# Sharing the softmax exponentials between ScalarE and VectorE, and folding the spectral half along both axes

## The chip, the cores and the metric

The kernel runs on one core of a Trainium2 chip. The metric is device time of one execution in microseconds; the median of the runs counts.

## What is computed

Two independent halves are concatenated along the last axis (S = 2048 rows, D = 448 columns each, bf16):

```python
# half A: attention, 16 heads of 28
qkv = x @ wqkv;  q, k, v = split into 16 heads
p = softmax(q k^T * 28**-0.5);  o = p v;  a = o @ wo
# half B: a filter in the frequency domain
X = rfft2(x) ; X = X * (w_r + 1j*w_i) ; b = irfft2(X)      # X is (2048, 225)
out = concatenate([a, b], axis=-1)                          # (2048, 896)
```

In the attention half 16 heads x 2048 x 2048 exponentials are needed, 67 million. That is 1024 *units* of one head, 128 keys and 512 queries (128 partitions x 512 elements).

## The kernel before

**Attention.** Four groups `g` of four heads, four blocks `qc` of 512 queries, sixteen blocks `kc` of 128 keys. `emit_st` (L639) multiplies keys by queries for three units at once: three matmuls with 28 rows each, at row tiles 0, 32, 64 or 96 of the array, each into a PSUM bank of its own out of six; two triples are in flight. `emit_act` (L655) makes one ScalarE exponential over the three banks (128x1536) and writes bf16 to `ET`, a ring of five. `emit_pv` (L662) multiplies the exponentials of four heads by the values: four matmuls with 32 output columns each, at column tiles 0, 32, 64 and 96, accumulated over the 16 key blocks in the bank `ACC`. A column of ones in the values gives the softmax sums; `finish` (L680) copies `ACC` out on VectorE, gathers the sums on TensorE (L702), takes reciprocals (L689), spreads them (L691, L694) and normalises (L698). The output projection is `o_job` (L708, matmuls L711).

**Projections.** Queries and keys (L393) and values (L408) contract over D = 448 as 128 + 128 + 128 + 64 rows, so one matmul in four uses 64 rows. They need x transposed. The first 512 rows are transposed on TensorE (L299), the other 1536 by transposing DMAs (L269).

**Spectral half.** All transforms are matmuls with constant cosine and sine tables. Rows s and s+1024 are added and subtracted on GpSimd first (L358, L361), so even and odd frequencies have half-length sums. `s_job` (L464) transforms along s, `x_job` (L487) along d, `zmul` (L518 to L524, GpSimd) multiplies by W, `y_job` (L554) transforms back along d, `z_job` (L586) back along s. Each of the four takes 128 matmuls. `w_job` (L534) transposes W on TensorE in 64 matmuls, after strided loads into `Wst` (L333 to L347).

**Order of the work.** [...] A planner in the builder (the loop from L809) keeps a clock per engine, with a cost per instruction, and emits TensorE's instructions in one fixed order: a triple of units if its banks are free, a value group if its exponentials are ready, otherwise one step of the job (projection, spectral step or output step) with the smallest due time. Jobs use bank 7 alone until the exponentials are done. The engines then run these fixed orders in sequence and wait on semaphores. If the key or query projection that a triple needs is not done, `force_until` runs it whole, ahead of everything.

The softmax here doesn't subtract the row's maximum and nothing guards it: scores larger than these inputs give would overflow.

## Time and profile before

Median of three runs: 563.34 us (560.5 to 572.84). The profiled execution took 570.4 us.

| engine | busy us | share of the span | instructions |
|---|---|---|---|
| TensorE (PE) | 500.1 | 88% | 3276 matmuls |
| ScalarE (ACT) | 473.6 | 83% | 352 |
| VectorE (DVE) | 132.4 | 23% | 218 |
| GpSimd (POOL) | 87.1 | 15% | 87 |

"Busy" is time in which the engine has an instruction in execution. A busy TensorE is not one at full speed: its clock is granted by a throttle, and the mean grant over this span was 0.844. The chain of work that ended last runs for 44% of the span on TensorE, 28% on ScalarE and 13% on DMA.

### The profile page before, as it was taken

What the parts mean: (1) busy time and instruction counts of PE and PEld (TensorE: products, weight loads), DVE (VectorE), ACT (ScalarE), POOL (GpSimd) and SP (SyncE); (2) the same over time, 40 slices, a digit from 0 to 9 for tenths busy, and PEclk for the clock granted to TensorE, in tenths of its full rate; (3) what the DMA queues carried; (4) which work ended last, traced back from release to release, by engine and by line L of the source; (5) the groups of instructions that cost most, each with busy time, mean ns of one, the idle gap of its engine ahead of it and who ended that gap; (6) DMA issues with size and microseconds to landing.
All of it is one profiled execution on the core that took longest, in us unless ns stands there. A gap on an engine that the chain in (4) does not pass through costs nothing.

```text
span 570.4 us, 7748 instructions
## 1 busy us (share of the span) xinstructions
PE 500.1 (88%) x3276; PEld 164.7 (29%) x3276; DVE 132.4 (23%) x218; ACT 473.6 (83%) x352; POOL 87.1 (15%) x87
## 2 busy tenths in 40 slices
PE   7699795999999999989999899999978888788786
PEld 3222232223333233333333222222222222222222
DVE  2111332212212222122211211213132122222323
ACT  2667895869999999999988579889977559899894
POOL 5038000000000000582505555000000000000000
PEclk9555755659999999999968659789999669999999
DMA  6492130000022022000000000000000011301012
GB/s 167 87 302 81 43 95 16 2 1 0 1 75 75 2 72 75 1 0 2 1 1 0 1 0 1 2 0 1 1 0 1 1 53 55 106 17 41 24 34 80
DMA packets 21394, 21.69 MB, mean 38 GB/s; under 512 B 11792, under 2 KB 19472, under 8 KB 20848
## 3 DMA queue, kind: packets, MB, share of 16 engines
q1 hardware_dynamic: 20208, 19.60, 11.8%
q10 hardware_dynamic: 960, 1.20, 0.7%
q0 software_dynamic: 192, 0.40, 0.3%
q8 instruction: 25, 0.41, 0.3%
q14 instruction: 9, 0.07, 0.1%
HBM read 15.95 MB, written 3.67 MB: 34 GB/s over the span
## 4 chain that ended last, share of the span: by engine, by line
PE 44%; ACT 28%; DMA 13%; issue 6%; DVE 6%; SPq 2%; DVEq 0%; ACTq 0%
ACT ET L659 28%; PE PS L649 11%; PE PS L670 8%; DMA Wst<-in_B_w_r_dram 6%; PE PS L554 5%; PE PS L393 4%; PE PS L487 4%; PE PS L586 3%; PE PS L408 3%; DMA Wst<-in_B_w_i_dram 3%; DMA xAT<-in_A_x_dram 3%; PE PS L464 2%; PE PS L711 1%; DMA R<-in_A_x_dram 1%; DVE R L569 1%
## 5 line engine op out<-in xcount | busy, mean ns | idle before, releaser
L659 ACT ACTIVATE ET<-PS 128x1536 bf16<-128x1536 f32 x342 | 467.3, 1611 | 79.0 <-PE PS L649 78.2
L649 PE MATMUL PS<-qT,kT 28*128 28x512 bf16 x1024 | 149.9, 435 | 26.3 <-ACT ET L659 16.0
L670 PE MATMUL PS<-ET,Vaug 128*32 128x512 bf16 x1024 | 115.4, 444 | 3.7 <-DVE Vaug L255 3.6
L649 PEld LDWEIGHTS PS<-qT,kT 28*128 28x128 bf16 x1024 | 33.6, 92 | 136.1 <-ACT ET L659 98.6
L670 PEld LDWEIGHTS PS<-ET,Vaug 128*32 128x32 bf16 x1024 | 26.5, 95 | 74.2 <-issue 68.4
L487 PE MATMUL PS<-R,T 112*113 112x512 bf16 (+1 forms) x128 | 45.6, 469 | 0.8 <-DVE Vaug L255 0.4
L518 POOL TENSOR_TENSOR ptmp<-R,WT 113x512 f32<-113x512 bf16 (+1 forms) x8 | 9.2, 1153 | 236.4 <-DVE R L500 236.4
L464 PE MATMUL PS<-FR,R 128*112 128x512 bf16 x128 | 39.8, 409 | 1.4 <-DVE R L468 0.5
L554 PE MATMUL PS<-T,R 113*128 113x448 bf16 (+1 forms) x128 | 34.7, 379 | 1.8 <-DVE R L569 0.8
L586 PE MATMUL PS<-R,FR 128*128 128x448 bf16 x128 | 35.1, 391 | 0.9 <-DVE R L569 0.5
L408 PE MATMUL PS<-wst,xAT 128*128 128x112 bf16 (+1 forms) x256 | 33.1, 242 | 2.8 <-DVE astg L598 0.8
L393 PE MATMUL PS<-xAT,wk 128*128 128x512 bf16 x64 | 25.5, 481 | 8.0 <-DMA xAT<-in_A_x_dram 5.6
L393 PE MATMUL PS<-xAT,wq 128*128 128x512 bf16 x64 | 23.3, 451 | 5.1 <-DVE astg L598 1.3
L500 DVE CAST R<-PS 113x512 bf16<-113x512 f32 (+1 forms) x16 | 11.1, 692 | 62.8 <-PE PS L487 33.5
L408 PEld LDWEIGHTS PS<-wst,xAT 128*128 128x128 bf16 (+1 forms) x256 | 18.1, 103 | 23.8 <-issue 8.8
L468 DVE CAST R<-PS 112x512 bf16<-112x512 f32 x16 | 11.1, 692 | 55.7 <-PE PS L464 55.7
L569 DVE CAST R<-PS 128x448 bf16<-128x448 f32 x16 | 10.0, 625 | 52.7 <-PE PS L554 44.1
L487 PEld LDWEIGHTS PS<-R,T 112*113 112x113 bf16 (+1 forms) x128 | 15.4, 151 | 19.5 <-issue 12.5
L255 DVE CAST Vaug<-PS 128x448 bf16<-128x448 f32 x16 | 10.0, 625 | 45.0 <-PE PS L408 45.0
L255 DVE CAST kT<-PS 128x512 bf16<-128x512 f32 x16 | 11.1, 691 | 40.2 <-PE PS L393 40.1
L534 PE MATMUL PS<-cid,Wst 128*113 128x128 bf16 (+1 forms) x64 | 10.8, 307 | 10.5 <-DMA Wst<-in_B_w_i_dram 8.7
L464 PEld LDWEIGHTS PS<-FR,R 128*112 128x112 bf16 x128 | 14.0, 133 | 17.9 <-issue 10.8
(57 smaller groups left out, 263.7 us busy)
## 6 DMA issues: line engine op xcount, KB each, us to landing
FR<-cst_f SPq DMA_DIRECT2D x4, 1024.0 KB, 8.4
FR<-cst_f SPq DMA_DIRECT2D x8, 512.0 KB, 3.6
out_dram<-astg SPq DMA_DIRECT2D x32, 112.0 KB, 1.7
R<-in_B_x_dram SPq DMA_DIRECT2D x2, 896.0 KB, 7.9
T<-cst_t SPq DMA_DIRECT2D x1, 896.0 KB, 4.7
T<-cst_t SPq DMA_DIRECT2D x1, 787.5 KB, 13.6
wst<-in_A_wqkv_dram ACTq DMA_DIRECT2D x1, 672.0 KB, 4.9
Wst<-in_B_w_r_dram SPq DMA_DIRECT2D x2, 225.0 KB, 9.9
```

The costliest lines, as they stand in the source:

```text
L255: P.op(eng, lambda e: e.tensor_copy(dst, src), reads=reads, writes=writes, cost=cost)
L393: mms.append(lambda e, M, c=c, rlo=rlo, rhi=rhi: e.matmul(M, wsb[rlo:rhi, c, g, :], xAT[rlo:rhi, c, 512 * n:512 * (n + 1)], start=(c == 0) ...
L408: mms.append(lambda e, M, c=c, rlo=rlo, rhi=rhi, kq=kq: e.matmul(M[:, 112 * kq:112 * kq + 112], xAT[rlo:rhi, c, 128 * (4 * n + kq):128 * ( ...
L464: mms.append(lambda e, M, c=c: e.matmul(M[0:112, :], src[:, c, 112 * b:112 * b + 112], F1v[:, i, c, :], start=(c == 0), stop=(c == 7)))
L468: P.op("dve", lambda e: e.tensor_copy(Sd[0:112, b, r, 512 * h:512 * h + 512], M[0:112, :]), reads=[mk], writes=[("Sd", h, r, b)], cost=0.68)
L487: mms.append(lambda e, M, ti=ti, part=part, v=v, q=q: e.matmul(M[0:kn, :], T1[0:112, v, q, k0:k0 + kn], Sd[0:112, q, part, 512 * h:512 * h ...
L554: mms.append(lambda e, M, ti=ti, sg=sg, p=p, v=v, b=b, kn=kn: e.matmul(M[:, 0:448], X[0:kn, b, sg, p, ks], T2[0:kn, v, b, :], start=(ti == ...
L569: P.op("dve", lambda e: e.tensor_copy(Y[:, t, r, :], M[:, 0:448]), reads=[mk], writes=[("Y", t, r)], cost=0.6)
L586: mms.append(lambda e, M, r=r, tt=tt, n=n: e.matmul(M[:, 0:448], F2v[:, a % 4, r, tt, :], Y[:, tt, r, :], start=(n == 0), stop=(n == 7)))
L649: ins = e.matmul(bank(u % 6), kT[32 * j:32 * j + DH, g % 2, 128 * kc:128 * (kc + 1)], qT[32 * j:32 * j + DH, g % 2, 512 * qc:512 * (qc + 1 ...
L659: P.op("act", lambda e: e.activation(ET[:, t % NE, 0:n], PS[:, b0:b0 + n], ACT.Exp, scale=scale), reads=[("B", u % 6) for u in us], writes ...
L670: ins = e.matmul(ACC[32 * j:32 * j + 32, :], Vaug[:, g % 2, kc, 32 * j:32 * j + 32], ET[:, t % NE, c0:c0 + 512], start=(kc == 0), stop=(kc ...
```

## The change

The builder is largely rewritten. What it changes on the chip:

1. **Exponentials on VectorE.** Of the 16 key blocks of every query block, blocks 3, 7 and 11 go to VectorE (192 of the 1024 units). The key projection is scaled so that a score arrives as 128 log2(e) times its value. VectorE adds a bias, clamps at zero and writes int16; read as bf16, these bits are a piecewise linear 2^x. Three more copies with 32, 64 and 96 added (shifts by 1/4, 1/2 and 3/4 of an octave) are averaged with it: values scaled by 2^(-c/4) (`Vs`) multiply copy c, so that TensorE sums four value products per such block. ScalarE keeps 13 blocks (832 units), in exponentials of three, two or one bank.
2. **Shared banks and a list scheduler.** All seven banks besides `ACC` serve units of either kind and jobs. VectorE and GpSimd instructions are queued and committed by due time; instructions [...] (`port=True`) are ordered against each other with semaphores.
3. **Column tiles.** Matmuls of jobs are issued as four matmuls of 32 output columns (`cols`), the form that the value products have, rather than one of 128.
4. **Projections** contract over 4 x 112 rows. All of x is loaded in plain layout and transposed on TensorE.
5. **Spectral half folded along both axes.** Rows s, 1024-s, 1024+s, 2048-s and columns d, 448-d are added and subtracted (`fold_chunk`), two chunks on GpSimd, two on VectorE; mirrored rows arrive by indirect DMA (`gather`). Each transform becomes a quarter of its size, with recombination in `zmul` (GpSimd) and `combine` (GpSimd).
6. **W in natural layout**: loaded with frequencies along partitions, the mirrored half with `gather`; no transposes on TensorE.

The aim is to take work from ScalarE and TensorE, at the price of more on VectorE and GpSimd. The core of the diff:

```diff
-        def emit_st(t):
-            us = units(t)
...
+        NB = 4 * NG
+        AQ, DQ = [], []
+        for b in range(NB):
+            for kc in range(16):
+                (DQ if kc in DKS else AQ).append((b, kc))
...
+        def mm(out, lhsT, rhs, start, stop):
+            def full(e):
+                return e.matmul(out, lhsT, rhs, start=start, stop=stop)
+            def cols(e):
+                m = out.shape[0]
+                for c in range(0, m, 32):
+                    c1 = min(c + 32, m)
+                    ins = e.matmul(out[c:c1], lhsT[:, c:c1], rhs, start=start, stop=stop, tile_position=(0, c))
+                return ins
+            return full, cols
...
+        def fill_dve(dsel):
+            for bk, (qi, b, kc, j, slot) in dsel:
+                P.defer("dve", lambda e, bk=bk, slot=slot: e.tensor_scalar(TT[:, 0, slot, :], bank(bk), BIAS, 0.0, ALU.add, ALU.max),
+                        reads=[("B", bk)], writes=[("T", slot)], busy=psum_cost(512), allow=0.8)
+                if slot % 2 == 1:
+                    for c in range(1, NW):
+                        P.defer("dve", lambda e, c=c, slot=slot: e.tensor_scalar(TT[:, c, slot - 1:slot + 1, :], TT[:, 0, slot - 1:slot + 1, :],
+                                                                                 SHF * c, None, ALU.add),
+                                reads=[("T", slot - 1), ("T", slot)], writes=[("T", c, slot // 2)], busy=0.336, allow=3.0, port=True)
...
+            P.op("act", lambda e: e.activation(dst, src, ACT.Exp, scale=ESC), reads=[("B", i) for i in o],
+                 writes=[("E", p + k) for k in range(n)], busy=0.4267 * n + 0.05)
...
+            ncop = 1 if kind == "A" else NW
+            for cc in range(ncop):
...
+                        lh = Vaug[:, g % 2, kc, 32 * j:32 * j + 32] if cc == 0 else Vs[:, g % 2, DKS.index(kc), cc - 1, 32 * j:32 * j + 32]
+                        ins = e.matmul(ACC[32 * j:32 * j + 32, :], lh, rhs, start=first, stop=last, tile_position=(0, 32 * j))
...
-                Wst[:, i, r, :, :], src[h:1024:2, :].rearrange("(t p) k -> p t k", p=128)),
+                P.dma("sp", lambda e, r=r, src=src: e.dma_start(Wn[:, t, 2 * r, :], src[lo:lo + 255:2, :]), "d_wb%d" % t, reads=wdep, writes=[("W", t, r)], kb=56)
+                gather(Wn[:, t, 2 * r + 1, :], src[:, :], 8 + t, "d_wr%d" % t, [("Wr", t, r)], 56, wdep)
...
-        for n, lo, hi in ((1, 512, 1024), (2, 1024, 2048)):
-            for c in range(4):
-                dlo = crow[c][2]
-                P.dma("sp", lambda e, lo=lo, hi=hi, c=c, dlo=dlo: e.dma_start_transpose(xAT[:, c, lo:hi], A_x[0][lo:hi, dlo:dlo + 128]),
+        for n in range(1, 4):
+            P.dma("sp", lambda e, n=n: e.dma_start(xa[:, n], A_x[0][512 * n:512 * n + 512, :].rearrange("(c p) d -> p c d", p=128)),
```

In the built program, TensorE's matmuls go from 3276 to 6268, of which 1024 are score matmuls (row tiles) before and after. Value products go from 1024 to 1600 (832 + 192 + 576). ScalarE has 121 exponentials of 1536, 224 of 1024 and 21 of 512 elements, in place of 341 of 1536 and one of 512. VectorE goes from 218 to 733 instructions, with 192 of the new 128x512 exponentials and 288 shifts of 128x1024 int16. TensorE's order changes between row tiles, column tiles and the full array 917 times before and 647 times after, 632 of these between row tiles and column tiles.

## The prediction

> **What bounds the kernel now.** I read first the page's slices, to see whether one limit holds all along.

> ```profile
> PE   7699795999999999989999899999978888788786
> ...
> ACT  2667895869999999999988579889977559899894
> ...
> PEclk9555755659999999999968659789999669999999
> ```

> It does not. Where PEclk is at 9, ScalarE is at 9; where it falls, ScalarE falls with it and TensorE stays full. The trace's clock has two values only, 1.00 and 0.50, so I asked for busy times in the stretches between its changes (microseconds, then busy with instruction starts for PE, PEld, DVE, ACT, POOL, then PEclk, DMA share, GB/s):

> ```profile
> 16.54:57.50 40.96, 36.03 (x181) 9.52 (x181) 5.33 (x8) 26.16 (x20) 17.81 (x18) 0.50 0.60 160
> ...
> 64.32:101.87 37.55, 27.59 (x168) 10.37 (x165) 9.68 (x14) 26.54 (x19) 0.00 (x0) 0.50 0.20 55
> ...
> 105.28:129.18 23.90, 23.42 (x122) 7.08 (x120) 3.32 (x5) 17.95 (x13) 0.00 (x0) 0.50 0.00 1
> 129.18:289.60 160.42, 147.66 (x1098) 53.20 (x1097) 38.95 (x62) 159.60 (x120) 30.66 (x28) 1.00 0.08 27
> ...
> 316.91:344.22 27.31, 27.21 (x117) 7.71 (x117) 4.14 (x7) 18.61 (x13) 13.33 (x13) 0.50 0.00 1
> ```

> At full clock ScalarE never stops: 120 exponentials in 160.42 us, 1.337 us each. At half clock TensorE never stops in the last row, and 13 exponentials take 27.31 us. Nine stretches at half clock make 177.5 us with 89 exponentials, which at 1.333 us would have needed 119: 59 us lost. So the span is 14 us start + 342 x 1.333 = 456 + 10 us tail + 59 half clock + some 32 lost at full clock (waits for loads; projections forced ahead of a triple) = 571.

> What trips the clock? I summed, over windows of 3.41 us from the first change, each matmul's columns streamed times its active share of the array (rows x columns of 128x128; a 28-row tile taken as 32), as a share of what the full clock could do. All nine falls follow a window of 0.29 to 0.42, all nine recoveries one of 0.71 to 0.90 of the *half* clock's capacity, 0.36 to 0.45 of the full one. A window with less than about 0.4 of the array's work costs half the clock until one comes with more.

> The costs, from the page's groups and the order of time:

> ```profile
> L659 ACT ACTIVATE ET<-PS 128x1536 bf16<-128x1536 f32 x342 | 467.3, 1611 | 79.0 <-PE PS L649 78.2
> L649 PE MATMUL PS<-qT,kT 28*128 28x512 bf16 x1024 | 149.9, 435 | 26.3 <-ACT ET L659 16.0
> L670 PE MATMUL PS<-ET,Vaug 128*32 128x512 bf16 x1024 | 115.4, 444 | 3.7 <-DVE Vaug L255 3.6
> ...
> L468 DVE CAST R<-PS 112x512 bf16<-112x512 f32 x16 | 11.1, 692 | 55.7 <-PE PS L464 55.7
> ```

> ```profile
> 180.07 0.39 PE L649 MATMUL PS<-qT,kT 28*128 28x512 bf16 x3
> 180.39 0.40 PE L670 MATMUL PS<-ET,Vaug 128*32 128x512 bf16 x4
> 180.72 0.85 PE L464 MATMUL PS<-FR,R 128*112 128x512 bf16 x3
> 181.50 0.39 PE L649 MATMUL PS<-qT,kT 28*128 28x512 bf16 x3
> ```

> Starts matter, since durations overlap: three row tiles, or four column tiles, take 0.32 to 0.33 us including one change of tiling; three full matmuls 0.78. A pass of 512 columns is 0.213, a change about 0.11. VectorE's 692 ns copies start 0.607 apart when back to back.

> [...]

> **The change, part by part.**

> *ScalarE.* 832 units x 0.427 (1.333 less about 0.05 fixed, over three) + 366 x 0.05 = 374 us, 82 less than 456. Smaller instructions cost only their fixed part, if TensorE is ahead.

> *TensorE at full clock.* Score passes: one per exponential, 366 x 0.213 = 78; VectorE's units mostly ride as a further row tile. Value passes 1600/4 x 0.213 = 85, up from 55. Changes 632 x 0.11 = 70, down from 101 (917). Query and key projections 128 x 0.213 = 27. Values: 256 passes of 112 columns, between 0.047 (112 columns) and 0.10 (L408 now, 9 in 1.03 us, with changes for the 64-row chunk that the change removes): 20. Spectral: 68 + 68 passes of 512, 64 of 225, 64 of 448 and small ones = 50, against 106 plus W's transposes. Output 12, normalising 8, transposes 4, warm-up 7. Sum 361, against some 415 by the same prices. Unknown is whether column tiles hide the loads of their weights at small N; at worst 0.05 on about 600 such passes, +30.

> *VectorE.* Exponentials 192 x 0.607 = 117. [...] 288 x 0.34 = 98. Copies out of PSUM 103 x 0.607 + 60 x 0.54, and folds (12 of about 1 us), reciprocals and small ones: 123. Sum 338, up from 132; beside ScalarE's 374 it fits, with little room. Every value product of a VectorE block waits for the exponential and three shifts, and all of TensorE's later work is queued behind it.

> *GpSimd.* `zmul` 8 x (12 x 0.6 + 4 x 1.08) = 92, from the 1.15 us of 113x512 now; folds 24, `combine` 19, 24 gathers about 20: 155, up from 87. It ends beside attention, as `i_job` is due 0.58 and later. [...] No transfer adds: the waits for transposing loads and W, which start the first stretches at half clock, go.

> *Clock.* Array work, by the same sum: scores 55, values 85 (from 55), projections 34, spectral 41 (from 96), the rest 23: 238, from 258. Over 450 us that is 0.53 on average, from 0.45, further from 0.4. The three early stretches (102 us) followed waits for loads; I keep 25. Of the six later ones (75 us) I keep 50. At half clock TensorE needs 2 x 291 + 70 = 652 for ScalarE's 374, so each such us loses 1 - 374/652 = 0.43: 75 x 0.43 = 32.

> *Sum.* 14 + 374 + 10 + 32 + 20 (lost at full clock: fewer loads awaited, but TensorE at 361 and VectorE at 338 beside 374) = **450 us**.

> **Rivals.**
> - *The engines don't mesh*: VectorE and GpSimd take turns at the port, value products come late, TensorE idles, windows fall under 0.4. For: three engines within 10%, a fixed order. Against: few semaphores per exponential. With 200 us at half clock, 86 lost, 10 more for turns: 14 + 374 + 10 + 86 + 10 = 494.
> - *It meshes*: hardly any half clock. For: 160 us of the kernel before, at 147.66 busy, lost nothing. Against: the stretches without spectral work (0.44 to 0.58) hold 0.47. 14 + 374 + 10 + 12 = 410.
> - *Slower*: [...] VectorE then needs 338 + 288 x 0.8 = 568, and 24 for start and tail: 592. [...]

> **How the numbers follow.** Forecast 0.55, not meshing 0.25, meshing 0.13, slower 0.05; 0.02 for a standstill at 563. Faster by over 2%: 0.93; within: 0.02; slower: 0.05. The range takes in meshing and not meshing with the +30 of small passes halved: 408 to 510.

> **What would show it.** Right: at full clock ScalarE saturated; half clock under 100 us; shifts about 0.34 apart; changes still 0.11. Wrong: shifts over 0.5; VectorE the engine waited for at value products; over 150 us at half clock; passes of column tiles slower than 0.213.

## The result, and the profile after

The changed kernel takes 469.12 us (median of 4 runs, 466.21 to 472.34), beside 568.09 us (560.5 to 577.63) for the kernel before on the same chip: a ratio of 0.837, with a 95% interval of 0.829 to 0.844. Some executions of either kernel run in a slower state, with a lower mean grant and a few per cent more time (the traced execution before, of 570.4 us, and that of e1 below are such), so every ratio in this document compares the faster ones alone and need not be the quotient of the two medians. The forecast was 450 us, the range 408 to 510. So direction and size were right, and the forecast was 19 us low.

The page's slices of the changed kernel, as shown of the kernel before:

```profile
PE   6999878798978999999689798886879999999996
...
ACT  2557828899999989998889978899787999999971
...
PEclk9579857899999999999879967798666999999999
```

PEclk and ACT are low together in most slices from 2 to 8 and from 20 to 31; in between and after, PEclk is at 9 and ACT at 8 or 9, up to the tail. The stretches between changes of the clock, those from 226 to 359 us put together in two rows (columns as before: length, busy time with instructions for PE, PEld, DVE, ACT, POOL, then PEclk, DMA share, GB/s):

```profile
55.70:76.18 20.48, 16.56 (x147) 4.27 (x151) 15.77 (x35) 8.61 (x10) 4.52 (x3) 0.50 0.00 1
...
93.25:226.37 133.12, 122.75 (x2177) 45.62 (x2169) 119.06 (x250) 126.18 (x123) 33.24 (x46) 1.00 0.09 24
226.37:267.32 40.95, 32.48 (x421) 9.92 (x421) 29.80 (x64) 38.05 (x37) 23.55 (x35) 0.88 0.01 2
267.32:359.49 92.17, 76.71 (x914) 22.53 (x910) 56.38 (x122) 78.43 (x70) 45.83 (x71) 0.72 0.01 2
359.49:448.00 88.51, 86.63 (x1379) 28.37 (x1371) 73.70 (x152) 85.36 (x84) 20.05 (x16) 1.00 0.07 23
```

From 93 to 226 us and from 359 us on, three engines run side by side and ScalarE is busy 95 and 96% of the time: this is what the change was to bring. From 226 to 359 us it is busy 87% of the time, with eight spells at half clock. The page's groups:

```profile
L925 ACT ACTIVATE ET<-PS 128x1024 bf16<-128x1024 f32 (+2 forms) x366 | 388.2, 1162 | 51.2 <-PE PS L896 48.8
...
L935 DVE TENSOR_SCALAR TT<-PS 128x512 int16<-128x512 f32 x192 | 130.6, 686 | 51.4 <-PE PS L896 50.1
L940 DVE TENSOR_SCALAR TT<-TT 128x1024 int16<-128x1024 int16 x288 | 106.0, 421 | 5.5 <-POOL ptmp L545 3.2
```

ScalarE's exponentials fall from 467.3 to 388.2 us busy. The shifts take 421 ns each; three of them back to back take 1.09 us (below, at 63.12), so they start about 0.34 us apart.

**Where the time went.** An exponential takes 0.427 us per bank and 0.053 fixed (back to back, exponentials of three, two and one bank start 1.330, 0.903 and 0.494 us after one another in the changed kernel's trace). The sum of that is ScalarE's own time; what the interval from the first exponential to the end of the last has beyond it is lost, at half clock or at full clock by where it lies. Where the clock changes between two exponentials, another way of dividing moves some 4 us from one of these to the other, and their sum stays. "At half clock" counts that interval alone. So every span is start + ScalarE + lost at half + lost at full + tail:

| profiled run | span | start | ScalarE | at half clock | lost there | lost at full | tail |
|---|---|---|---|---|---|---|---|
| before | 570.4 | 13.8 | 455.1 | 177.5 | 68.2 | 22.5 | 10.8 |
| changed | 468.4 | 15.5 | 374.5 | 98.2 | 38.9 | 25.2 | 14.3 |
| e1 all exponentials on ScalarE | 565.7 | 13.4 | 459.1 | 346.8 | 76.1 | 5.1 | 11.9 |
| e2 no port order | 515.3 | 13.6 | 375.5 | 157.4 | 71.3 | 43.8 | 11.1 |
| e3 dummies | 465.1 | 13.6 | 374.9 | 64.9 | 29.8 | 36.2 | 10.6 |
| e4 full tiles | 505.1 | 13.5 | 374.4 | 167.3 | 57.9 | 35.0 | 24.4 |
| e5 same order, no port order | 498.3 | 13.7 | 374.5 | 129.7 | 49.3 | 46.9 | 13.9 |
| e6 same order, full tiles | 478.0 | 13.2 | 374.5 | 119.5 | 44.1 | 32.8 | 13.4 |
| e7 slack | 478.4 | 13.7 | 374.8 | 122.9 | 44.7 | 33.9 | 11.3 |
| e8 slack and dummies | 463.6 | 13.5 | 374.9 | 64.9 | 26.6 | 36.2 | 12.5 |
| e9 changed, another chip | 500.2 | 13.1 | 374.5 | 139.9 | 65.4 | 32.9 | 14.3 |
| e10 slack and dummies, that chip | 476.1 | 13.0 | 374.9 | 61.4 | 41.1 | 37.5 | 9.6 |
| e11 no low window, that chip | 484.7 | 13.4 | 375.5 | 61.4 | 41.2 | 41.4 | 13.2 |
| e12 e1 with dummies, that chip | 536.0 | 13.5 | 456.5 | 99.2 | 45.7 | 9.2 | 11.2 |

Of the 102 us between the first two rows, 80.6 are ScalarE's own sum, 29.3 half clock; full clock, start and tail give 8 back. But the first row is long for its kernel. The shorter executions of the kernel before, beside the experiments, take 554 to 563 us with mean grants of 0.854 to 0.877, which is 137 to 164 us at half clock in place of 177.5. Against those the gain is some 91 us, and ScalarE's 80.6 leave some 10 for the clock and all else, an estimate from these spans.

Two places stand out in the changed kernel. The first is early. The order of time from 58 us:

```profile
58.80 4.11 POOL L545 TENSOR_TENSOR R1b<-wst 128x896 bf16<-128x896 f32 x2 [2.69 <-DVE TT L940]
...
63.01 0.20 DVE L515 TENSOR_SCALAR Vs<-Vaug 128x128 bf16<-128x128 bf16 x1 [1.90 <-POOL R1b L545]
63.12 1.09 DVE L940 TENSOR_SCALAR TT<-TT 128x1024 int16<-128x1024 int16 x3
63.59 0.11 PEld L992 LDWEIGHTS PS<-TT,Vs 128*32 128x32 bf16 x4 [3.52 <-DVE TT L940]
63.59 1.47 PE L992 MATMUL PS<-TT,Vs 128*32 128x512 bf16 x12 [3.01 <-DVE TT L940]
```

A 0.2 us scaling of the values waits its turn in the order that the program's semaphores set among instructions with `port=True` (turns at "the port", the program's word, from here on), until two folds on GpSimd (4.11 us) are through. The shifts are queued behind it on VectorE, the value product waits for the shifts, and all of TensorE's later work waits behind the value product: 3.01 us in which the array does nothing. From 60 to 80 us ScalarE loses 9.6 us, the most of any 20 us. Not all of it is the wait's: the clock had already fallen at 55.70 us, after a window with 0.35 of the array's work.

The second is the stretch from 226 to 359 us. GpSimd's instructions on the tile `ptmp`, its scratch in `zmul`, from 200 us on:

```profile
L545 POOL TENSOR_TENSOR R1a<-ptmp x32: 571/582/592, 212.6 to 353.4; 128x225 bf16<-128x225 f32 x32
...
its engine sat idle before it (us, times) until:
  DVE TT L940: 54.5, 28
  DVE Vs L515: 10.5, 7
```

`zmul` runs until 354 us, although its work is 91 us by the same view: for 65 us of it GpSimd waits for VectorE's turn at the port. The backward transforms need all of it and start at 360 us. From 217 us, the last `x_job`, to 360 us TensorE has no spectral work at all.

### The profile page after: what moved, and what is told of

Same layout as the page of the kernel before. It is cut to its first block, busy times and chain, and to the rows that moved or that the text cites. A ratio compares the mean times of both kernels' runs of the same rounds, so it can differ in the third digit from the quotient of the medians.

```text
span 468.4 us, 14535 instructions
## 1 busy us (share of the span) xinstructions
PE 412.5 (88%) x6268; PEld 144.3 (31%) x6268; DVE 352.1 (75%) x733; ACT 393.7 (84%) x374; POOL 165.8 (35%) x203
## 4 chain that ended last, share of the span: by engine, by line
PE 37%; ACT 26%; DVE 14%; POOL 11%; issue 7%; DMA 2%; SPq 0%; ACTq 0%; DVEq 0%; POOLq 0%
ACT ET L925 26%; PE PS L992 14%; PE PS L896 11%; PE PS L442 11%; DVE TT L940 4%; DVE TT L935 4%; POOL R1b L540 3%; POOL ptmp L545 3%; POOL wst L545 2%; POOL R1b L545 2%; DVE onrm L545 2%; DMA cid<-cst_id 2%; PE PS L459 1%; DVE oaug L1051 1%; POOL R1a L545 1%
## 5 line engine op out<-in xcount | busy, mean ns | idle before, releaser
L925 ACT ACTIVATE ET<-PS 128x1024 bf16<-128x1024 f32 (+2 forms) x366 | 388.2, 1162 | 51.2 <-PE PS L896 48.8
L935 DVE TENSOR_SCALAR TT<-PS 128x512 int16<-128x512 f32 x192 | 130.6, 686 | 51.4 <-PE PS L896 50.1
L940 DVE TENSOR_SCALAR TT<-TT 128x1024 int16<-128x1024 int16 x288 | 106.0, 421 | 5.5 <-POOL ptmp L545 3.2
L992 PE MATMUL PS<-ET,Vaug 128*32 128x512 bf16 x832 | 89.0, 425 | 6.9 <-ACT ET L925 6.2
L992 PE MATMUL PS<-TT,Vs 128*32 128x512 bf16 x576 | 48.6, 449 | 3.2 <-DVE TT L940 3.2
L545 POOL TENSOR_TENSOR ptmp<-ptmp,R1b 128x450 f32<-128x450 f32 x32 | 31.6, 1007 | 11.4 <-DVE TT L940 10.5
L545 POOL TENSOR_TENSOR ptmp<-R1a 128x225 f32<-128x225 bf16 (+2 forms) x36 | 25.1, 715 | 28.5 <-DVE TT L940 15.7
L442 PE MATMUL PS<-T,R 112*32 112x448 bf16 (+4 forms) x512 | 26.9, 309 | 0.3
L992 PE MATMUL PS<-TT,Vaug 128*32 128x512 bf16 x192 | 22.2, 452 | 0.5 <-DVE oaug L1051 0.5
L442 PE MATMUL PS<-wv,xAT 112*32 112x112 bf16 x1024 | 21.3, 228 | 0.1
## 6 DMA issues: line engine op xcount, KB each, us to landing
FR<-cst_tab SPq DMA_DIRECT2D x3, 1024.0 KB, 10.6
```

The lines of the kernel that those rows point to most:

```text
L442: ins = e.matmul(out[c:c1], lhsT[:, c:c1], rhs, start=start, stop=stop, tile_position=(0, c))
L545: P.defer(eng, lambda e: e.tensor_tensor(out, a, b, op), reads=reads, writes=writes, busy=c, allow=allow, port=True, after=after)
L925: P.op("act", lambda e: e.activation(dst, src, ACT.Exp, scale=ESC), reads=[("B", i) for i in o], writes=[("E", p + k) for k in range(n)], ...
L935: P.defer("dve", lambda e, bk=bk, slot=slot: e.tensor_scalar(TT[:, 0, slot, :], bank(bk), BIAS, 0.0, ALU.add, ALU.max), reads=[("B", bk)], ...
L940: P.defer("dve", lambda e, c=c, slot=slot: e.tensor_scalar(TT[:, c, slot - 1:slot + 1, :], TT[:, 0, slot - 1:slot + 1, :], SHF * c, None, ...
L992: ins = e.matmul(ACC[32 * j:32 * j + 32, :], lh, rhs, start=first, stop=last, tile_position=(0, 32 * j))
```

## The experiments

e1 to e8 ran on one chip, beside 561.66 and 562.55 us for the kernel before; e9 to e12 on another, beside 563.12 us. The changed kernel is not the same on all chips (469 us above, 505 us on the second; see e9), so every ratio below is to the kernel before on the same chip, and runs are compared on their own chip. For e1 to e8 the changed kernel itself was not run again. e5 and e6 keep its order and lose before 40 us and from 180 to 220 us what it lost (8.7 and 6.6, 8.3 and 5.2, against 8.8 and 5.7 us), so nothing of what sets e9 apart is in them, and the changed kernel's 0.837 is taken to hold there too, which is an inference. Differences below are worked out from the ratios where these and the medians differ.

### e1: the exponentials stay on ScalarE

```diff
-DKS = (3, 7, 11)
+DKS = ()
...
```

> All exps on ScalarE (no column block on VectorE, no shifts, no scaled values); the rest of the change is kept and the scheduler plans anew. Theory (the move of the exps is what shortens the path, and TensorE's clock follows how much array work there is per microsecond): ScalarE's own sum goes from 374 back to 457 us; the array's work falls by the 576 extra value groups (some 31 us) and is spread over a longer span, about 0.38 per microsecond, below the 0.4 under which the clock fell, so more half clock than the 98 us of the changed kernel: 150 us or more with 60 to 70 us lost; 15 + 457 + 14 + 65 + 10 = 560 us, no better than the kernel before by more than 3%. Rival (the clock is no matter of array work; the losses stay as in the changed kernel, 39 + 25): 550 us with about 100 us at half clock. Rival (TensorE's relief brings the gain, the exps are secondary): below 530 us.

Measured: 559.69 us, a ratio to the kernel before of 0.996 (0.994 to 0.999). The first theory's 560 holds.

```profile
PE   7798988888987889998898889889889998889976
...
ACT  2579899898888988789989899997998889888892
...
PEclk9588699695577765555555597995655568585776
```

TensorE has less work than in the changed kernel, yet PEclk is at 5 or 6 in 23 of the 40 slices: 347 us at half clock. The traced execution is the longest of the four (567.55 us, mean grant 0.686); the others have 0.709 to 0.719, which is 314 to 324 us at half clock. The work that is left is spread too thinly: with dummies added and the planner number of e7 (e12), half clock falls to 99 us. So everything else in the change, the folded spectral half, the shared banks, the column tiles and W in natural layout, gives 0.4% by itself in the order that this planner makes, and the move of the exponentials makes the difference. How much of that is the clock, e12 asks.

### e2 and e5: no order at the port

e2 leaves out the semaphores between VectorE's and GpSimd's instructions with `port=True` and lets the planner know it; e5 leaves out the semaphores alone, so that every engine's order stays the changed kernel's own.

```diff
-        self._emit_waits(eng, reads, writes, self.port[1] if port and self.port[0] not in (None, eng) else None)
+        self._emit_waits(eng, reads, writes, None)
...
-        return self.port[2] if self.port[0] not in (None, eng) else 0.0
+        return 0.0
```

(The second pair is in e2 alone.)

> The semaphores that make VectorE's shifts and folds and GpSimd's folds and products take turns are left out, and the scheduler plans without them; nothing else. Theory (the turns stretch GpSimd's 92 us of products to 150 us and hold VectorE up at 63 us, and both lower TensorE's array work below 0.4): GpSimd's products end at about 300 us rather than 353, the transforms back start by then, half clock after 220 us falls from 64 us to 30 or less, the 9.6 us wait at 63 us shrinks: 450 to 458 us. Rival ([...]the waits move into the instructions themselves): shifts of VectorE or products of GpSimd take more than 1.3 times as long, 465 to 480 us. Rival (the waits cost nothing): 466 to 471 us with the same half clock.

> The changed kernel's own order of instructions, kept on every engine; only the waits that make VectorE and GpSimd take turns at the port are not issued (79 of them), so the planner's choices do not differ as in e2. In e2 the 64 shifts that met a GpSimd operation took 1.08 us in the mean, the 224 others 0.42. Theory (such a meeting holds VectorE up for the rest of GpSimd's run of operations, and the ordered turns are the cheaper of the two): shifts again over 0.5 us in the mean, VectorE awaited more, half clock above 120 us, 480 to 510 us. Rival (e2 was slow because its new order was bad, not because of the meetings): 462 to 472 us.

Measured: e2 517.13 us (ratio 0.923, 0.918 to 0.928), e5 502.56 us (0.894, 0.886 to 0.902). The first theory of e2 falls: taking away the waits costs 48 us, and 32 us with the order kept, as e5's theory had it. VectorE's groups of e5, then of e2:

```profile
L940 DVE TENSOR_SCALAR TT<-TT 128x1024 int16<-128x1024 int16 x288 | 143.7, 550 | 0.3
L515 DVE TENSOR_SCALAR Vs<-Vaug 128x128 bf16<-128x128 bf16 x36 | 14.4, 412 | 0.2
```

```profile
L940 DVE TENSOR_SCALAR TT<-TT 128x1024 int16<-128x1024 int16 x288 | 150.4, 565 | 0.5
L515 DVE TENSOR_SCALAR Vs<-Vaug 128x128 bf16<-128x128 bf16 x36 | 17.8, 496 | 0.4
```

The idle time before the shifts is gone (0.3 us against 5.5), but they themselves take 143.7 us against 106.0. By the times of start and end, 64 of e5's 288 shifts met an array operation of GpSimd: these took 1.01 us in the mean and up to 4.57, the other 224 took 0.42. VectorE's exponentials, which read PSUM, took 0.68 whether they met one or not. These 64 account for all the time by which the shifts are longer. Of them, 58 met two operations of GpSimd and took 0.92 us in the mean; the longest met six, of which five ended before it did. So the shifts are held up where they meet GpSimd and the exponentials from PSUM are not; three shifts (one in e5, two in e2) were held through five to nine instructions in a row. What holds them, the traces do not show. What the order written out with semaphores changes is who waits: in the changed kernel GpSimd, 65 us in `zmul`; in e5 VectorE, on whose shifts the value products wait and all of TensorE's later work. `zmul` ended early, at 298 us in e5 and 318 us in e2, and it did not help: the backward transforms began at 382 and 352 us, where TensorE's order has them.

### e3: work for the sake of the clock

24 dummy jobs of four passes of 512 columns, whose results nobody reads, due where TensorE has no spectral work.

```diff
+        def filler(i, due):
+            def mms(M):
+                return [mm(M, wq[0:112, 0, 0, :], xAT[0:112, 0, 0:512], c == 0, c == 3) for c in range(4)]
+            add(("fl", i), due, [("xAT", 0, 0), ("wq0", 0)], mms, lambda M, mk: None)
+        for i in range(24):
+            filler(i, NA * (0.46 + (0.76 - 0.46) * (i + 0.5) / 24))
```

> 24 dummy jobs of 4 column-tile passes of 512 (16 matmuls of 112 rows by 32 columns, 0.87 us each, results never read) due between 0.46 and 0.76 of the exps, that is from about 215 to 355 us, where TensorE has no spectral work; the rest is planned by the same scheduler. Theory (array work below 0.4 per microsecond is what lowers the clock): the 64 us of half clock between 220 and 360 us fall to 20 or less, and the 20 us lost there to 8; TensorE's extra 21 us of passes and 22 changes of tiling fit into its idle time: 455 to 462 us. Rival (the clock does not follow array work): 64 us of half clock stay, and the dummies take time from the pairs of scores: 475 us or more. Rival (the clock recovers, but TensorE is short of time): half clock 20 us, time 466 to 475.

Measured: 465.61 us (0.827, 0.821 to 0.833), against the changed kernel's 0.837 (0.829 to 0.844). Between 220 and 360 us, first the changed kernel, then e3:

```profile
220.00:360.00 140.00, 114.62 (x1420) 34.29 (x1412) 92.11 (x198) 122.77 (x110) 73.22 (x112) 0.78 0.01 2
```

```profile
220.00:360.00 140.00, 129.42 (x1965) 41.55 (x1953) 101.97 (x217) 132.43 (x125) 74.69 (x114) 0.95 0.01 2
```

With 545 more matmuls TensorE is granted 0.95 instead of 0.78, and ScalarE does 125 exponentials instead of 110. The clock did what the theory said (14 us at half clock in this stretch, before 61), and the stretch gained 9 us. The whole gained only some 5, and the intervals overlap: from 360 us on, e3 loses 8 us more than the changed kernel, in an order that the planner made anew. e7 and e8 ask the question with less of that.

### e4 and e6: full tiles instead of column tiles

e4 lets the planner know, e6 keeps the changed kernel's order and issues each pass of a job as one full-array matmul. First e4's edit, then e6's:

```diff
         def add(name, due, needs, mms, end, n=512, full=False, deps=()):
+            full = True
...
```

```diff
-            pe_op(m, f[0] if jb.full else f[1], jb.needs, [("B", bk)], jb.n / 2400.0 + 0.004)
+            pe_op(m, f[0], jb.needs, [("B", bk)], jb.n / 2400.0 + 0.004)
```

> Every projection, transform and output job as full-array matmuls in place of four column tiles, as in the kernel before; the scheduler's order then has 771 changes of tiling where it had 647. Theory (a change costs about 0.11 us of an idle array): 124 x 0.11 = 14 us more for TensorE, of which half falls on the path: 473 to 482 us. Rival (column tiles bring nothing, their passes only cost issue time): 460 to 469 us.

> The changed kernel's own order kept; every pass of a projection, transform or output job issued as one full-array matmul in place of four column tiles. Changes of tiling go from 647 to 798. Theory (151 changes at 0.10 to 0.14 us, the gaps of 0.316 to 0.354 from end to end against 0.215 without a change, are 15 to 21 us of idle array; about half lies where TensorE sets the pace): 476 to 484 us with half clock about 110 us. Rival (the idle array also pulls windows below 0.4): half clock above 140 us, 490 to 508 us, like e4. Rival (e4 was slow because of its new order alone): 466 to 473 us.

Measured: e4 504.19 us (0.898, 0.893 to 0.904), e6 487.91 us (0.862, 0.852 to 0.872; 480 to 502 in single runs). By the ratios the column tiles are worth some 14 us in the same order (0.862 against 0.837). TensorE is busy 432.8 us against 412.5: 20 us more with 151 more changes of tiling, 0.13 each, inside the 0.10 to 0.14 expected, though more half clock is in it too. e6's profiled run of 478.0 us is the quickest of its runs and divides its 10 us over half clock (+5) and full clock (+8). By its ratio e6 takes some 484 us, the upper edge of the first theory; its median lies between the two theories. More than half of e4's loss (35 us by the ratios) is the new order: there the first transforms end at 217 us instead of 181, everything spectral comes later, and the tail grows to 24 us.

### e7 and e8: one planner number, with and without dummies

e7 changes one number of the planner, and e8 adds 16 of e3's dummies, due between 0.46 and 0.76.

```diff
-        TH, SLACK, JLEAD = 0.75, 0.12, 24
+        TH, SLACK, JLEAD = 0.75, 0.25, 24
```

> One number of the scheduler: a job's pass may now delay the next pair of scores by 0.25 us in its plan, before 0.12, so that TensorE leaves fewer gaps; nothing else. Theory (TensorE's idle time between scores is what lowers the clock early and what squeezes the jobs at the end): the planned span falls by 8 us and the planned windows with array work below 0.39 go from 19 to 16: 452 to 462 us. Rival (ScalarE waits more often for late scores): 468 us or more, with ScalarE's waits at full clock above 30 us.

> e7 with 16 of e3's dummy jobs due between 0.46 and 0.76 of the exps (14 us of passes whose results are not read). Planned windows with array work below 0.39: 7, planned span 442 us. Theory (clock follows array work): half clock below 60 us, and 8 to 12 us less than e7: 444 to 453 us. Rival (as in e3, what the clock gains is taken back by later stages): within 4 us of e7.

Measured: e7 480.86 us (0.857, 0.853 to 0.862), e8 463.52 us (0.826, 0.820 to 0.832). e7 missed: a plan 8 us shorter made a run 12 us longer, with 123 us at half clock. The planner's own clock of TensorE is always the full one, which may be why. Against e7, e8 is 17 us shorter, and the dummies are the only edit: up to 220 us the two lose the same (38.2 and 38.4 us beyond ScalarE's own time), and ScalarE's exponentials come in the same order and sizes until 232 us. From 220 to 360 us, e7 and then e8:

```profile
220.00:360.00 140.00, 121.10 (x1500) 35.97 (x1497) 92.16 (x197) 121.07 (x111) 74.21 (x115) 0.73 0.01 2
```

```profile
220.00:360.00 140.00, 125.63 (x1925) 41.07 (x1922) 102.21 (x220) 131.28 (x123) 75.43 (x116) 0.92 0.01 2
```

That is the cleanest test of the clock in this study: 14 us of useless work shorten the kernel by 17. Half clock in this stretch falls from 75 to 22 us, and 11 of the 15 us between the two traced executions lie here. The rival (taken back later) falls. One reservation stays: around the dummies the planner places the other work anew, and no run put dummies into an order that was otherwise kept.

### e9 to e12: the changed kernel again, two versions meant to beat it, and e1 with dummies

e10 is e8 with these numbers and 56 dummies of two passes each; e11 has 42 of four passes in other places, and planner numbers of its own; e12 is e1 with e7's number and 80 dummies of four passes. In these three, and in e4, an output copy goes to ScalarE only when its slot is free. In e10:

```diff
-                  sem, reads=["idx"] + list(rd), writes=writes, kb=kb, issue=1.1)
+                  sem, reads=["idx"] + list(rd), writes=writes, kb=kb, issue=1.25)
...
-        TH, SLACK, JLEAD = 0.75, 0.12, 24
...
+        for n, lo, hi in ((8, 0.19, 0.25), (48, 0.44, 0.78)):
...
+        TH, SLACK, JLEAD = 0.75, 0.3, 24
```

> The changed kernel, unedited, beside e10 to e12 for a comparison on one chip. All theories: 465 to 472 us, half clock 80 to 110 us.

> A version meant to beat both kernels, made from e7 and e8: jobs may delay the scores by 0.30 us in the plan, the plan's cost of a gather's issue on GpSimd is 1.25 us in place of 1.10 (the trace of e8 has 0.95 to 1.09 us each with 0.30 between them, and a scaling of the values waited 2.88 us at 195 us for a turn that the plan had put too early), and 56 dummy jobs of 2 passes (0.43 us each), 8 due between 0.19 and 0.25 of the exps and 48 between 0.44 and 0.78. Planned span 442 us with 3 windows of array work below 0.39 (e8: 442 with 7). Theory (the clock follows array work): half clock 25 to 45 us, 20 us or less lost to it, 450 to 459 us. Rival (the ends of stages and the turns at the port set a floor that dummies do not move): 461 to 466 us, like e8.

> 42 dummy jobs of 4 passes (36 us of TensorE's time; 8 due between 0.02 and 0.09, 2 between 0.19 and 0.25, 32 between 0.48 and 0.72 of the exps), jobs may delay the scores by 0.20 us, and pairs are placed when ScalarE has 0.80 us left in place of 0.75. Planned span 449 us with no window of array work below 0.39. Theory (the clock follows array work): half clock 30 us or less, the least of all runs, yet more of ScalarE's wait at full clock because TensorE is short of time: 453 to 463 us. Rival (the half clock of the early stage comes from VectorE's waits and stays): half clock before 110 us above 25 us.

> e1 (all exps on ScalarE) with the scheduler's 0.25 us as in e7 and 80 dummy jobs of 4 passes (70 us of TensorE's time) between 0.08 and 0.95 of the exps. It separates what the move of the exps gave by shortening ScalarE's sum (459 to 375 us) from what it gave by keeping TensorE at full clock: e1 was at half clock for 347 us. Planned span 492 us with 5 low windows. Theory (both matter; the dummies mend the clock and leave the longer sum): 13 + 459 + 12 and 20 to 30 lost, 504 to 514 us, half clock below 80 us. Rival (dummies cannot mend it, TensorE has no room): 540 us or more.

Measured: e9 505.29 us (0.903, 0.895 to 0.912), e10 478.22 us (0.858, 0.852 to 0.865), e11 485.05 us (0.869, 0.860 to 0.878), e12 539.34 us (0.966, 0.958 to 0.975).

**e9** was the surprise: the same program, 36 us longer than in the result, while the kernel before took what it took elsewhere. From 180 to 220 us, first the changed kernel on the chip of the result, then e9:

```profile
180.00:220.00 40.00, 38.83 (x818) 16.87 (x814) 34.60 (x76) 37.39 (x37) 29.39 (x41) 1.00 0.28 75
```

```profile
180.00:220.00 40.00, 22.94 (x375) 8.68 (x372) 17.81 (x38) 18.55 (x19) 15.45 (x16) 0.70 0.27 74
```

Half of everything, with the same traffic. The order of time in e9 shows how:

```profile
196.49 0.61 PE L896 MATMUL PS<-qT,kT 28*128 28x512 bf16 x3 [3.78 <-issue]
...
203.57 0.69 DVE L935 TENSOR_SCALAR TT<-PS 128x512 int16<-128x512 f32 x1 [7.23 <-remote]
203.63 1.02 ACT L925 ACTIVATE ET<-PS 128x1024 bf16<-128x1024 f32 x1 [8.99 <-remote]
204.32 0.52 PEld L442 LDWEIGHTS PS<-T,R 113*32 113x32 bf16 x16 [7.18 <-DVE TT L935]
```

While the table for the backward transforms and W are loaded (from 188 us), TensorE, ScalarE and VectorE stand still together, for 3.8 and then some 7 us; the trace names no instruction on the core that they wait for ("issue", "remote"). The same happens once before 40 us, while x is loaded, and at both places in e10, e11 and e12. These two places cost e9 40.3 us and the changed kernel in the result 14.5, which is 26 of the 36 us. The records of q8, the larger of the two queues that the page marks `instruction`, allow a guess: in the changed kernel's profile its packets come at 188.8, 193.7, 199.7, 204.3 and 214.2 us, in e9 at 187.7 and then only at 215.0. Instructions may have come late behind the loads; the programs with more matmuls have more such packets (49 on the changed kernel's page, 30 on e4's and 25 on that of the kernel before, with 6268, 3796 and 3276 matmuls). No run tested this, and the changed kernel was traced once on either chip, so the cause stays open.

**e10** is the version that beats both kernels: 0.858 against e9's 0.903 on the same chip, 27 us less, and by the ratio some 79 us less than the kernel before. From 220 to 360 us it is granted 0.99 (e9: 0.84), and does 128 exponentials (115). Its 450 to 459 us were missed, because the stops before 40 and after 180 us cost it 38.3 us; with the 14.5 that these places cost the changed kernel in the result it would be some 454, an estimate. e10 changes more than the dummies, so its 27 us are not theirs alone.

**e11** has 61 us at half clock, of which 51 lie at the two stops: elsewhere 10 us, the least of all runs. But 36 us of dummies leave more lost at full clock (41.4 us) than e10 has, and 7 us more in all. The clock obeyed, and the price seems to have been too high; as e11's planner numbers differ from e10's too, that is not shown.

**e12** has 99 us at half clock in place of e1's 347. Its time missed the expected 504 to 514 and is all but the rival's 540; yet 35.7 us of its 54.9 lost lie at the two stops (before 40 us, and from 160 to 200 us), and elsewhere ScalarE is held up by 19 us in all. Without them, and with what e1 lost at these places (16.4 us), it would be some 520 us, an estimate from these sums. So, by this estimate, much of the clock could have been mended without moving the exponentials; what the move gives that nothing else here gives is ScalarE's 80 us.

## Why the prediction was right, and where it was off

The sum was right because its large term was, ScalarE's own time, and because the rule of the clock held; the time at half clock was in part a guess. Every other term was too small, so nothing cancelled: the profiled run's 18.4 us over the forecast are 1.5 (start) + 0.5 + 4.3 (tail) + 6.9 (half clock) + 5.2 (full clock). The half clock has 12 us more than allowed for in the early stage and 11 more from 226 to 359 us; e8 shows that the low windows of that stretch can be filled. The runs that made `zmul` itself earlier with the exponentials on VectorE (e2, e5) did other harm.

## What to carry to other kernels

When one engine is the bound and TensorE feeds it, look at TensorE's clock first: what counted in these traces is the array's work per window, and a stretch with too little of it can cost more than the work that would fill it (17 us against 14 in e8); e11, with 36 us of such work, took 7 us more than e10 with 24. Spread the work that can be moved over such stretches; make a planner count windows, not only microseconds. Where instructions of two engines hold each other up when they meet, as VectorE's shifts and GpSimd's array operations did (1.01 us for a shift in place of 0.42 in e5), order their turns in short runs, let the one wait on whom least depends, and count those turns in the duration of the slower engine.

## What was not expected of the hardware

- Useless matmuls made the kernel faster: 14 us of them took 17 us off (e8 against e7), and on the second chip 24 us of them, with two planner numbers and another rule for output copies, took 27 us off (e10 against e9).
- A VectorE shift that met an array operation of GpSimd took 1.01 us in the mean in place of 0.42 (e5); three were held for a run of five to nine operations, up to 4.57 us in e5 and 5.48 us in e2.
- The same program took 469 us on one chip and 505 us on another, with three engines standing still for up to 9 us during a burst of loads, while the kernel before differed by 1% between them; why is open.
